# Loads of q and k: a fourth buffer, and issue 1.6 steps earlier

## The chip, the core and the metric

The kernel runs on one core of one Trainium2 chip. The metric is the device time of one execution in microseconds, as the median of several runs. Five engines work side by side, each with its own instruction queue in order: TensorE (PE, with its weight loads PEld), VectorE (DVE), ScalarE (ACT), GpSimd (POOL) and SyncE (SP), which computes nothing here and issues the plain transfers between HBM and the on-chip memory. Engines wait for one another through semaphores.

## The reference, cut to what matters

Attention in two forms is added up, and its result goes through a layer of eight experts, of which each token uses one.

```python
q, k, v: [8 batches, 8 heads, 576 tokens, 64]
q_d, k_d, v_d = means over 4 neighbouring tokens          # 144 tokens
out_d   = softmax(q_d k_d^T / 8) v_d, each row repeated 4 times
out_loc = softmax(q k^T / 8, only where |i - j| < 4) v
x = (out_d + out_loc) as [4608 tokens, 512]
e = argmax(x w_gate + bias);  out[t] = gate[t] * relu(x[t] w1[e]) w2[e]
```

## The kernel before

**Attention.** The work is cut into 32 steps (`N = 4 * B`), one for each pair of heads of a batch: step n is batch n // 4, pair n % 4. A step transposes q and k on PE (`tp`, line 278; `tpt`, line 291, for the remainder of two steps together), copies them on ACT (`qT`, `kT`), computes the banded scores in blocks (`sc`, line 341) and the pooled scores (`scd`, line 368), takes maxima and sums on DVE, exponentials on ACT and the normalizing products on POOL (`nl`, line 395; `nd`, line 399). The weights are transposed (`pdt`, line 417, on PE; `lt` on DVE) and multiplied with v: `avd` (line 431) with the pooled v, `avl` (line 446) with v itself. The pooled v comes from `vp` (line 266) on PE, once for two steps. `X` (line 457) adds both parts on DVE.

**Routing.** After each batch but the last, gate logits, the argmax and each token's place in a table are computed (`Router`), the table is written by indirect transfers of POOL (`scatter`, line 603), and the rows of x are turned by DVE (`R`, line 588) and stored to a buffer xs in HBM by SP (`store`, line 597). From the first four batches a first unit of 512 tokens is gathered while attention still runs (`entries`, line 834; `gather`, line 844).

**Experts.** From about 280 us on the experts' matrix products follow (lines 892 and 940), with weights loaded by SP (`wload`, lines 794 and 796).

**The order of the work** is written out by hand. Each operation has a phase in the table `PHASE`, in steps: operation x of step n is due at n + PHASE[x], so `vp` of step 4 is due at 4 + 2.4192. `build` collects all calls with their due times through `call(at, f, ...)`, sorts them by due time, and issues them in that order under a manual schedule; each engine works through its own instructions in this order. A due time is thus a place in an order, not a time on a clock.

**The loads.** `load_qk` (line 225) loads q and k of four heads of one batch, two steps' worth, with number h = 2 * batch + half: two transfers for q and two for k, 288 KB each, in rows of 256 bytes, all issued by SP at line 234. Its tiles `qt` and `kt` each hold 9 x 2 x 64 words a partition and rotate through a number of buffers; a load waits until the transposes that read the old content of its buffer are done. The loads h = 0, 1 and 2 stand ahead of everything; h = 3 to 15 come from the schedule (line 1022). `load_v` (line 237) loads v of four heads of the next batch into one of two v tiles, as four transfers of 192 KB (line 254), two such halves a batch (line 1020). SP also issues two fills of buffers in HBM at the start (`Router.start`, due at step 2.55: `xs<-zr` at line 476 and `tab<-ft`, 324 KB, at line 480) and the stores of the rows of x. All these stand in one queue, SP's.

The due times of SP's work around the change, with `last` = 0.1888 and `used` = 3.5377: v's halves of batch b+1 at 4b + 2.84 and 4b + 3.64, load h of q and k at 2h - 4.56, the stores of batch b at 4b + 8.17, 4b + 8.55 and 4b + 10.55.

Of the kernel before, what the change touches and what calls it, by code (L numbers as in the profile page):

```python
# [7 lines left out]
F32 = mybir.dt.float32  # L8
# [9 lines left out]
B, H, S, D = 8, 8, 576, 64  # L18
# [178 lines left out]
class Attention:  # L197
# [27 lines left out]
    def load_qk(s, b, half):  # L225
        nc = s.nc

        qt = s.ld.tile([128, 9, 2, D], F32, name="qt", bufs=3)
        kt = s.ld.tile([128, 9, 2, D], F32, name="kt", bufs=3)
        for j in (slice(0, 5), slice(5, 9)) if (b, half) == (0, 0) else (slice(0, 9),):  # L230
            for t, src in ((qt, s.q), (kt, s.k)):
                for a in range(2):
                    h = src[b, 4 * half + 2 * a : 4 * half + 2 * a + 2].rearrange("h s d -> (h s) d")
                    nc.sync.dma_start(t[:, j, a], h.rearrange("(j p) d -> p j d", p=128)[:, j])
        s.QK[2 * b + half] = (qt, kt)
# [717 lines left out]
def build(tc, q, k, v, mid, w_gate, bias, w1, w2, out):  # L953
    nc = tc.nc
    with ExitStack() as ctx:
# [8 lines left out]
        with ExitStack() as actx:  # L964
# [6 lines left out]
            at = Attention(tc, actx, ectx, C, ps, q, k, v)  # L971
# [27 lines left out]
            def call(at, f, *args):  # L999
                calls.append((at, len(calls), f, args))  # L1000
# [3 lines left out]
            last = max(P["tpq"], P["tpk"], P["tpt"])  # L1004
# [14 lines left out]
                    for j in range(2):  # L1019
                        call(4 * b - 1 + used + 0.3 + 0.8 * j, at.load_v, b + 1, 4 * j)  # L1020
            for h in range(3, N // 2):
                call(2 * h - 5 + last + 0.25, at.load_qk, h // 2, h % 2)


            call(0.95, C.sums, nc)
# [202 lines left out]
```

## Time and profile before

| What | us |
|---|---|
| runs before: median of 3 | 731.39 |
| runs before: lowest, highest | 731.2, 736.78 |
| the profiled execution: its own time | 737.82 |
| its span in the trace | 735.8 |
| busy in the span: PE | 670.7 |
| DVE, ACT, POOL | 381.1, 358.3, 296.9 |

The profile is of one execution. The span runs from its first to its last instruction. "Busy" is the time in which an engine works on an instruction; the durations of PE's products are modelled, and they overlap. In a row of the timeline there stand the start in us, the duration, the engine ("SPq" for a transfer that SP issues, with the time that the issuing takes), the line, the operation, what it writes and reads, and how many instructions were merged; in brackets follows the idle time before it and what ended this. The rows of stretches give the busy time of each engine in the stretch, the clock granted to PE as a share of full speed, the mean busy share of the sixteen DMA engines, and the rate.

### The profile page before, as it was taken

The numbers are of one execution on the slowest core, as the hardware profiler recorded it, in microseconds if no ns is written. First come the engines' busy times: TensorE is split into PE (matmuls) and PEld (weight loads), VectorE is DVE, ScalarE is ACT, GpSimd is POOL, SyncE is SP. The second block draws the span as 40 slices with busy tenths as digits, with TensorE's granted clock in tenths as the row PEclk, the third lists the DMA queues.
The fourth block names the chain that finished last, engine by engine and source line by source line (L and its number), as shares of the span: only waits on it lengthen the run. The fifth ranks groups of instructions, "written<-read, shape, count | busy, mean of one in ns | idle before, by whom it ended". The sixth has DMA issues, their size and how long they took to land. (4 is left out here: it accounts for less than half of the span.)

```text
span 735.8 us, 19186 instructions
## 1 busy us (share of the span) xinstructions
PE 670.7 (91%) x7467; PEld 540.8 (73%) x7467; DVE 381.1 (52%) x877; ACT 358.3 (49%) x804; POOL 296.9 (40%) x390
## 2 busy tenths in 40 slices
PE   6899989898869788894999999999999999999994
PEld 4677767676747566683788888888888888889793
DVE  3578778597737596650743423435224353235720
ACT  3688778676646474530443432434314343235620
POOL 6757585657767658066313132131412102211101
PEclk9899999999988999997899999999999999999998
DMA  9899778798997936936356253561635424344800
GB/s 177 159 188 169 175 153 176 143 192 181 175 169 126 163 85 131 299 95 184 129 135 210 61 145 138 141 203 46 187 112 155 160 78 146 106 144 139 252 14 28
DMA packets 175711, 107.92 MB, mean 147 GB/s; under 512 B 135582, under 2 KB 154050, under 8 KB 175619
## 3 DMA queue, kind: packets, MB, share of 16 engines
q1 hardware_dynamic: 167362, 87.45, 51.6%
q0 software_dynamic: 8256, 19.22, 8.4%
q8 instruction: 60, 0.98, 0.7%
q14 instruction: 33, 0.26, 0.1%
HBM read 87.39 MB, written 19.51 MB: 145 GB/s over the span
## 5 line engine op out<-in xcount | busy, mean ns | idle before, releaser
L944 POOL DMA_INDIRECT out_dram<-o,tg x37 | 40.1, 1083 | 258.9 <-ACT o L943 210.5
L821 DVE TENSOR_TENSOR wlo<-raw,whi 128x1024 fp32r<-128x1024 f32 x72 | 86.8, 1234 | 92.8 <-ACT whi L815 89.1
L897 DVE SCALAR_TENSOR_TENSOR hl<-l,hh 128x512 fp32r<-128x512 f32 x72 | 49.7, 690 | 106.6 <-ACT hh L896 104.2
L940 PE MATMUL l<-whi,hh 128*128 128x512 f32 x256 | 100.3, 396 | 0.0
L940 PE MATMUL l<-whi,hl 128*128 128x512 f32 x256 | 99.7, 390 | 0.0
L940 PE MATMUL l<-wlo,hh 128*128 128x512 f32 x256 | 99.6, 390 | 0.0
L896 ACT ACTIVATE hh<-l 128x512 fp32r<-128x512 f32 x72 | 42.6, 597 | 117.1 <-PE l L892 106.7
L892 PE MATMUL l<-xh,whi 128*128 128x512 f32 (+1 forms) x256 | 96.0, 377 | 2.1 <-DVE mni L623 1.1
L892 PE MATMUL l<-xl,whi 128*128 128x512 f32 (+1 forms) x256 | 95.2, 372 | 0.0
L892 PE MATMUL l<-xh,wlo 128*128 128x512 f32 (+1 forms) x256 | 95.0, 372 | 0.0
L815 ACT CAST whi<-raw 128x1024 fp32r<-128x1024 f32 x70 | 70.7, 1050 | 30.1 <-issue 12.0
L943 ACT ACTIVATE o<-l,tg 128x512 f32<-128x512 f32 x37 | 25.4, 687 | 110.4 <-PE l L940 58.2
L341 PE MATMUL sc<-kT,qT 64*24 64x32 f32 x3072 | 45.4, 194 | 16.9 <-issue 16.3
L411 ACT COPY Pw<-lt 32x288 f32<-32x288 f32 x128 | 54.6, 426 | 8.8 <-DVE lt L406 6.7
L341 PEld LDWEIGHTS sc<-kT,qT 64*24 64x24 f32 x3072 | 35.1, 100 | 31.4 <-issue 26.7
L892 PEld LDWEIGHTS l<-xh,whi 128*128 128x128 f32 x256 | 48.3, 189 | 12.2 <-issue 3.4
L940 PEld LDWEIGHTS l<-wlo,hh 128*128 128x128 f32 x256 | 48.1, 188 | 10.2
L603 POOL DMA_INDIRECT tab<-ig,si x36 | 37.9, 1053 | 42.8 <-DVE mbase L738 17.8
L940 PEld LDWEIGHTS l<-whi,hh 128*128 128x128 f32 x256 | 48.0, 188 | 9.6
L940 PEld LDWEIGHTS l<-whi,hl 128*128 128x128 f32 x256 | 48.1, 188 | 9.5
L892 PEld LDWEIGHTS l<-xl,whi 128*128 128x128 f32 x256 | 48.5, 190 | 8.3 <-issue 0.4
L892 PEld LDWEIGHTS l<-xh,wlo 128*128 128x128 f32 x256 | 48.5, 190 | 8.3
(246 smaller groups left out, 1315.0 us busy)
## 6 DMA issues: line engine op xcount, KB each, us to landing
raw<-in_moe_w_dram SPq DMA_DIRECT2D x176, 128.0 KB
raw<-in_moe_w_dram SPq DMA_DIRECT2D x44, 512.0 KB
vw<-in_v_dram SPq DMA_DIRECT2D x53, 192.0 KB
qt<-in_q_dram SPq DMA_DIRECT2D x30, 288.0 KB
kt<-in_k_dram SPq DMA_DIRECT2D x30, 288.0 KB
xs<-R SPq DMA_DIRECT2D x64, 128.0 KB
vw<-in_v_dram SPq DMA_DIRECT2D x15, 96.0 KB
xs<-R SPq DMA_DIRECT2D x12, 64.0 KB
```

Source lines behind the costliest of these rows:

```text
L341: s.nc.tensor.matmul(p[32 * j : 32 * j + SUB, i, :], qT[r, q0 : q0 + SUB], kT[r, q0 : q0 + WIN], start=False, stop=(i == NB - 1), skip_gro ...
L411: s.nc.scalar.copy(s.Pw[n % NPW][r, :, j, :SUB], s.t["lt", n][r, :, :SUB])
L603: i = nc.gpsimd.indirect_dma_start(out=s.tab[:, :], out_offset=bass.IndirectOffsetOnAxis(ap=C.si[:, t : t + 1], axis=0), in_=C.ig[:, t, :] ...
L815: (nc.gpsimd.tensor_copy if turn <= 4 else nc.scalar.copy)(hi, raw)
L821: (nc.gpsimd if 2 < turn <= 4 else nc.vector).tensor_tensor(lo, raw, hi.bitcast(F32), op=ALU.subtract)
L892: nc.tensor.matmul(p[:, f % n, :], a[:, fs], x[:, k, :N], start=(k == 0 and i == 0), stop=(k == 3 and i == 2))
L896: nc.scalar.activation(hh[:, g, :N], p, AF.Relu)
L897: nc.vector.scalar_tensor_tensor(hl[:, g, :N], p, 0.0, hh[:, g, :N].bitcast(F32), op0=ALU.max, op1=ALU.subtract)
L940: nc.tensor.matmul(p, a[:, f, hs], x[:, f % 2, :], start=(f == 0 and i == 0), stop=(f == 7 and i == 2))
L943: nc.scalar.mul(o, p, T[:, h, 1:2].bitcast(F32))
L944: nc.gpsimd.indirect_dma_start(out=s.out[:, :], out_offset=bass.IndirectOffsetOnAxis(ap=T[:, h, 0:1], axis=0), in_=o, in_offset=None, boun ...
```

## The change

`qt` and `kt` get four buffers each, and the due time of load h (h = 3 to 15) goes from 2h - 5 + `last` + 0.25 to 2h - 6.6 + `last` + 0.25. The transposes that use load h begin at step 2h. Nothing else is changed: the same transfers, of the same size, by the same engine.

```diff
     def load_qk(s, b, half):
         nc = s.nc
 
-        qt = s.ld.tile([128, 9, 2, D], F32, name="qt", bufs=3)
-        kt = s.ld.tile([128, 9, 2, D], F32, name="kt", bufs=3)
+        qt = s.ld.tile([128, 9, 2, D], F32, name="qt", bufs=4)
+        kt = s.ld.tile([128, 9, 2, D], F32, name="kt", bufs=4)
...
             for h in range(3, N // 2):
-                call(2 * h - 5 + last + 0.25, at.load_qk, h // 2, h % 2)
+                call(2 * h - 6.6 + last + 0.25, at.load_qk, h // 2, h % 2)
```

## Prediction

> **What bounds the kernel now.** I began with the page's busy shares and cut the attention stage (0 to 280 us) into stretches of 40 us, because the change touches only that stage. Columns: stretch, its length, busy time of PE, PEld, DVE, ACT and POOL with their instruction counts, granted clock, DMA share, GB/s.
>
> ```profile
> 40.00:80.00 40.00, 38.20 (x942) 30.02 (x940) 30.62 (x93) 32.29 (x98) 27.48 (x41) 1.00 0.92 170
> 80.00:120.00 40.00, 37.73 (x922) 29.25 (x917) 31.42 (x100) 30.95 (x98) 24.45 (x36) 1.00 0.80 172
> 200.00:240.00 40.00, 31.87 (x663) 24.94 (x658) 23.09 (x70) 23.00 (x70) 27.14 (x37) 0.83 0.83 149
> ```
>
> From 40 to 120 us PE has 1.8 and 2.3 us idle in 40: it sets the pace. The DMA engines are 80 to 92% busy beside it. So there are two limits that lie close together, and the question is whether PE ever waits for a load. The views of the tiles kt and of the line that pools v (L266) answer it with everything that PE waited for on loads in the whole attention stage; the tile qt shows no wait for a DMA.
>
> ```profile
>   DMA kt<-in_k_dram: 3.1, 1
> ...
>   DMA vw<-in_v_dram: 2.3, 1
> ```
>
> These are two waits. The timeline of PE places them, both in the first 20 us, on loads that the change leaves alone:
>
> ```profile
> 15.71 0.52 PE L278 MATMUL tp<-ident,kt 128*128 128x128 f32 x3 [3.11 <-DMA kt<-in_k_dram]
> ...
> 20.02 1.50 PE L266 MATMUL vp<-vw,pool 128*32 128x256 f32 x9 [2.33 <-DMA vw<-in_v_dram]
> ```
>
> Next the timeline of SyncE, which issues every load (start, duration, line, what, how many):
>
> ```profile
> 7.07 2.46 SPq L234 DMA_DIRECT2D kt<-in_k_dram  x2
> ...
> 12.81 3.60 SPq L254 DMA_DIRECT2D vw<-in_v_dram  x5
> ...
> 30.79 1.02 SPq L234 DMA_DIRECT2D qt<-in_q_dram  x2
> 31.91 3.85 SPq L234 DMA_DIRECT2D kt<-in_k_dram  x2
> 35.86 1.08 SPq L476 DMA_DIRECT2D xs<-zr  x1
> 37.04 0.59 SPq L480 DMA_DIRECT2D tab<-ft  x1
> 37.68 4.51 SPq L254 DMA_DIRECT2D vw<-in_v_dram  x4
> 42.29 3.08 SPq L234 DMA_DIRECT2D qt<-in_q_dram  x2
> 45.47 2.87 SPq L234 DMA_DIRECT2D kt<-in_k_dram  x2
> 48.39 4.50 SPq L254 DMA_DIRECT2D vw<-in_v_dram  x4
> ```
>
> The rows follow one another without a gap. SyncE is never ahead of its plan and waiting for a buffer; it is behind, and each issue takes as long as the queue needs to accept it. So in this stage **a place in the order of SyncE's queue is worth time, and a due time in steps is not**.
>
> **What the change moves.** Call a load of q and k "qk" with its number h (four transfers of 288 KB), and the two halves of v for batch b "vA(b)" and "vB(b)" (four transfers of 192 KB each). The largest of the three PHASE values that `last` takes is 0.1888, so a qk load was due at step 2h-4.56 and is now due at 2h-6.16. vA(b+1) is due at 4b+2.84, vB(b+1) at 4b+3.64, the fills of xs and tab at 2.55, the stores of the rows at 0.17, 0.55 and 2.55 of each four steps.
>
> qk3 goes from 1.44 to -0.16, but nothing else on SyncE stands between these, and it already follows directly on the loads of the constants: no change, cost nothing. qk4 goes from 3.44 to 1.84: it passes the two fills and vA(1), its four issues with it. In every later round the even qk passes a row store and vA, the odd qk passes two row stores. vB keeps the same set of transfers ahead of it. The added buffers mean 9 KB more a partition (two of 9x2x64 words), and a wait for buffer h-4 instead of h-3. The buffer was free long before in either case: qk4 was issued at 42.29 although its old buffer's last transposes belong to step 3, done before 32 us.
>
> **Gain of having q and k earlier: nothing.** The only wait for them that the trace shows is the one at 15.71, which stays. Bound: 0 from both sides, since a load that nobody waits for can't be made worth more.
>
> **Cost of having vA later.** How long does a load take from the end of its issue until PE can use it? Two rows tell it: the kt load issued until 7.07+2.46 = 9.53 let PE go at 15.71, 6.2 us later; the group of v that ended by 12.81+3.60 = 16.41 let PE go at 20.02, 3.6 us later. vA(1) is issued until 37.68+4.51 = 42.19, so it lands between 45.8 and 48.4. Its user is the v pooling of step 6:
>
> ```profile
> 47.68 1.06 PE L266 MATMUL vp<-vw,pool 128*32 128x256 f32 x12
> ```
>
> That row shows no wait, so the room is between 0 and 1.9 us. I take 0.5: vA(1) follows large transfers (288 KB, and tab's 324 KB), as the kt load did, not small ones as the first v did, and is nearer to the 6.2.
>
> qk4 occupies the queue from 42.29 to 48.39, 6.1 us. With it ahead, vA(1) lands 6.1 us later and **PE waits 6.1 - 0.5 = 5.6 us at about 48 us** (4.2 to 6.1). PE works in order: behind the v pooling stand avd, scd, avl and the second scores of step 6, hence ACT's Od and exp, DVE's lm and X. All engines lose the same time.
>
> **The clock after it.** The closest case is PE's wait of 5.16 us at 213.83:
>
> ```profile
> 213.83 1.52 PE L417 MATMUL pdt<-ident,de 128*96 128x128 f32 x6 [5.16 <-POOL de L399]
> 215.13 0.37 PE L332 MATMUL sc<-mask,identb 128*128 128x192 bf16 x1
> 215.29 1.06 PE L278 MATMUL tp<-ident,qt 128*128 128x128 f32 x4
> ...
> 228.28 0.86 PE L417 MATMUL pdt<-ident,de 128*96 128x128 f32 x6
> ...
> 229.21 0.60 PE L278 MATMUL tp<-ident,qt 128*128 128x128 f32 x4
> ```
> ```profile
> 193.70:197.10 3.40, 2.93 (x14) 2.82 (x15) 0.89 (x2) 1.09 (x3) 3.13 (x6) 0.50 1.02 170
> 213.80:217.60 3.80, 3.77 (x20) 3.21 (x24) 2.45 (x7) 1.66 (x5) 3.44 (x5) 0.50 1.04 220
> ```
>
> After the wait the granted clock is 0.50 for 3.8 us: six pdt take 1.52 instead of 0.86, four transposes of q 1.06 instead of 0.60, and four of k as much again. Loss 0.66 + 0.46 + 0.46 = **1.6 us** (0 to 1.6). The page "TensorE: Matmul & The Clock Gate" of the Trainium skill (section "What's actually happening") says that half clock comes after at least one idle window of about 3.4 us; by it the short end of the stall, 4.2 us, need not hold a whole window and would cost no clock. The other half-clock row here follows an idle of only 2.2 us:
>
> ```profile
> 194.17 1.52 PE L417 MATMUL pdt<-ident,de 128*96 128x128 f32 x6 [2.20 <-POOL de L399]
> ```
>
> So the trace is stricter than the rule, and I keep the 1.6.
>
> **The later rounds.** The same reckoning for vA(3) and vA(4), the tightest ones:
>
> ```profile
> 90.15 3.94 SPq L254 DMA_DIRECT2D vw<-in_v_dram  x4
> 94.19 1.60 SPq L234 DMA_DIRECT2D qt<-in_q_dram  x2
> ...
> 102.46 5.19 SPq L254 DMA_DIRECT2D vw<-in_v_dram  x4
> ...
> 122.93 2.86 SPq L254 DMA_DIRECT2D vw<-in_v_dram  x4
> 125.89 3.77 SPq L234 DMA_DIRECT2D qt<-in_q_dram  x2
> ...
> 134.77 6.29 SPq L254 DMA_DIRECT2D vw<-in_v_dram  x4
> ```
> ```profile
> L266 PE MATMUL vp<-vw,pool x12: 376/379/403, 107.4 to 108.1; 128*32 128x256 f32 x12
> ...
> L266 PE MATMUL vp<-vw,pool x12: 376/379/403, 137.5 to 138.2; 128*32 128x256 f32 x12
> ```
>
> vA(3): issued until 94.1, plus the 8.3 us of qk8, plus 3.6 to 6.2, is 106.0 to 108.6 against a use at 107.4. vA(4): 125.8 + 8.9 + 3.6 to 6.2 = 138.3 to 140.9 against 137.5, late by 0.8 to 3.4. But by then PE is 5.6 us behind its old times while the queue, which does not wait for PE, is not: both are covered, and cost nothing. Without that cover they cost 0 to 1.2 and 0.8 to 3.4 us. The stall at 48 us therefore buys the room for all later rounds; and were it made up meanwhile, vA(4) would still hold PE back.
>
> **What is won back.** Early: PE idles 1.8 + 2.3 = 4.1 us between 40 and 120; if the other engines run ahead during the stall, some of that can close. Most of it is lockstep, so 1 us (0 to 4.1). Late: near 210 us POOL waits 6.0 us for a scatter that lands slowly beside the full queue, and PE shows gaps with no releaser near 220:
>
> ```profile
> POOL tg L834 <- DMA tab<-ig,si: 6.0, 1, 6.0
> ...
> 219.75 0.28 PE L341 MATMUL sc<-kT,qT 64*24 64x32 f32 x4 [0.51 <-issue]
> ```
>
> The queue's last v issues end at about 221; with PE some 6 us later this work meets an emptier queue. I take 1.5 us (0 to 4, two thirds of the scatter's wait).
>
> **Sum:** +5.6 + 1.6 - 1.0 - 1.5 = **+4.7 us**. Ends: 4.2 + 0 - 4.1 - 4 = -3.9, and 6.1 + 1.6 = +7.7. From 280 us on the expert stage follows the attention in one chain, so the loss is carried to the end. Against the profiled execution's own 737.82 us (span 735.8) that gives 742.5. That execution is 6.4 us above the median of the runs shown, 731.39, like one of these (736.78); to the median the same sum gives **736.1 us**.
>
> **Rivals.**
>
> A, the room holds: not slower, 731.4. The mechanism is the queue's lead over PE at step 6: vA(1) may land 6.1 us later without harm where the whole queue stands further ahead of PE than in this profile. It decides from a lead that is 4.2 us longer than here (landing at 47.68 - 6.1 = 41.6 of the old times, against 45.8 at best). Against it: the first 40 us are issued back to back, with nothing to shorten. For it: the profiled execution is itself 6.4 us above the median, and some of that may sit here. Chance 0.14. The page "DMA: Bandwidth & Descriptors" of the Trainium skill (section "Rules for kernel authors") advises to issue a DMA early, to compute meanwhile and to wait for it late; by it an earlier q and k can only help, which here means 731.4 at best, as the trace shows no wait for them after 15.71.
>
> B, faster: the qk loads are out of the queue earlier, SyncE catches up before 200 us and the scatter lands at once; the 5.16 us of PE and the 1.6 us of clock go, with no stall at 48: 731.4 - 6.8 = 724.6. Against it: ahead of the last row stores and v loads stands the same set of transfers as before, so the queue is as full at 209. Chance 0.08.
>
> C, more than one stall: if the queue slows together with PE, because the row stores wait for DVE's rows, vA(3) and vA(4) are late again: 5.6 + 1.6 + 0.6 + 2.1 = +9.9, 741.3. For it: every vA loses a place. Against it: SyncE is about a step behind its plan, so rows are ready. Chance 0.20.
>
> D, the change does not do what it says, in that q and k are no earlier, since the queue and not the due time sets their issue. The order of calls is the order of SyncE's rows, so I give it no chance of its own beyond qk3, where it is true.
>
> **How the numbers follow.** My forecast has 0.58, with its own range of 731 to 739. One per cent, 7.3 us, is about what a measurement of this kernel can tell from no change. Slower by more: C nearly whole (0.17) and the upper end of the forecast (0.10), 0.27. Faster by more: half of B and something unseen, 0.09. Within: 0.64. The range reaches from 728 (the sum's low end is 727.5) to 742 (C).
>
> **What would show it.** In the changed profile the four issues of qk4 stand ahead of the fills of xs and tab; the L266 row of step 6 carries a wait of 4 to 6 us for a DMA of vw, with a half-clock stretch behind it; no later L266 row waits more than 1 us; steps 7 to 24 begin some 5 us later than before; the transposes of q and k still wait for no load after 20 us. Wrong would be: no wait at the L266 row of step 6, or a span that shrinks while that wait is there.

## The result, and the profile after

| | before | with the change |
|---|---|---|
| median of 20 runs, us | 731.93 | 735.62 |
| lowest, highest | 722.34, 736.78 | 733.57, 741.51 |

The ratio is 1.0086, with a 95% interval of 1.0059 to 1.0113; it leaves out the runs more than 1.5% above the fastest run of the same kernel, which are nine of the 20 before and none of the change's, so it is larger than the quotient of the medians of all runs (1.0050). The change makes the kernel slower, by 0.5% by these medians and 0.9% by the ratio; in the repetition further down both agree on 0.8%. The forecast was 736.1 us.

SyncE's timeline of the changed kernel around the first moved load (start, duration, line, what, how many):

```profile
30.04 1.07 SPq L234 DMA_DIRECT2D qt<-in_q_dram  x2
31.15 3.12 SPq L234 DMA_DIRECT2D kt<-in_k_dram  x2
34.38 3.46 SPq L234 DMA_DIRECT2D qt<-in_q_dram  x2
37.94 2.82 SPq L234 DMA_DIRECT2D kt<-in_k_dram  x2
40.85 1.16 SPq L476 DMA_DIRECT2D xs<-zr  x1
42.10 0.58 SPq L480 DMA_DIRECT2D tab<-ft  x1
...
42.74 4.79 SPq L254 DMA_DIRECT2D vw<-in_v_dram  x4
```

qk4 (34.38 to 40.76) now stands ahead of the fills and of vA(1). vA(1) begins to issue at 42.74 where it began at 37.68: 5.1 us later. Its first user is the `vp` of step 4, due at 6.42 and therefore called the v pooling of step 6 here. PE's timeline shows what becomes of it:

```profile
46.83 0.63 PE L341 MATMUL sc<-kT,qT 64*24 64x32 f32 x48
51.66 1.93 PE L266 MATMUL vp<-vw,pool 128*32 128x256 f32 x12 [4.20 <-DMA vw<-in_v_dram]
53.52 1.23 PE L431 MATMUL avd<-PdT,vd 96*64 96x144 f32 x8
54.68 1.38 PE L368 MATMUL scd<-kd,qd 64*64 64x144 f32 x12
...
58.44 0.60 PE L278 MATMUL tp<-ident,qt 128*128 128x128 f32 x4
```

The v pooling of step 6, which had no wait before, waits 4.20 us for v. Its own work then takes 1.93 us instead of 1.06. Stretches of PE around it, with the granted clock third from the end:

```profile
48.80:51.60 2.80, 0.00 (x0) 0.00 (x0) 0.00 (x0) 0.10 (x1) 1.09 (x2) 0.50 0.81 159
51.60:55.60 4.00, 3.94 (x28) 2.34 (x30) 0.00 (x0) 0.72 (x3) 0.22 (x1) 0.50 1.24 225
55.60:60.00 4.40, 4.40 (x108) 3.67 (x108) 3.72 (x11) 3.05 (x11) 0.95 (x3) 1.00 1.21 218
```

The clock is at one half from 48.8 us, within the wait, and for 4 us after it. From the start of the pooling to the next transposes of q it takes 58.44 - 51.66 = 6.8 us. In the profile of before the same stretch runs from 47.68 to these transposes:

```profile
52.65 0.60 PE L278 MATMUL tp<-ident,qt 128*128 128x128 f32 x4
```

That was 5.0 us. So the stretch behind the wait takes 1.8 us more, which the half clock would explain (the filler below tests this), and wait and stretch together lose 6.0 us. The 40 us that hold both read accordingly:

```profile
40.00:80.00 40.00, 34.06 (x823) 26.42 (x823) 26.85 (x84) 27.23 (x85) 22.23 (x33) 0.91 1.01 184
```

PE is busy for 34.1 us in 40 where it was for 38.2. The loads do not stand still with it: the eight issues of vA(1) and vB(1) end at 51.5 us, where in the kernel before vB(1), behind the same set of transfers, ended at 52.9. The v poolings of batches 3 and 4, at 114.57 and 143.28, wait for nothing:

```profile
114.57 1.06 PE L266 MATMUL vp<-vw,pool 128*32 128x256 f32 x12
...
143.28 1.06 PE L266 MATMUL vp<-vw,pool 128*32 128x256 f32 x12
```

### The profile page after: what moved, and what is told of

It is laid out like the page before. It is cut to its first block, busy times and chain, and to the rows that moved or that the text cites. A ratio compares the mean times of both kernels' runs of the same rounds, so it can differ in the third digit from the quotient of the medians.

```text
span 733.5 us, 19178 instructions
## 1 busy us (share of the span) xinstructions
PE 671.2 (92%) x7467; PEld 541.1 (74%) x7467; DVE 381.7 (52%) x877; ACT 358.4 (49%) x804; POOL 298.4 (41%) x390
```

## The experiments

The theory: the loss is one wait, since vA(1) has no room at step 6 and stands behind one more load of q and k. The rivals: the buffers themselves; a small loss at each displaced half of v; a loss elsewhere, with the wait made up later. Each kernel was timed beside the kernel before on the same chip; the four of the first group shared one set of runs of it (median 725.40), the next four another (727.22), the last two a third (725.25).

**Four buffers alone.** The new due time is taken back, the buffers stay.

```diff
-                call(2 * h - 6.6 + last + 0.25, at.load_qk, h // 2, h % 2)
+                call(2 * h - 5 + last + 0.25, at.load_qk, h // 2, h % 2)
```

> Four buffers for q and k, with the old due times: SyncE's order is that of the kernel before. Theory (the loss is the first half of v for batch 1 standing behind one more load of q and k): the same time as before, within 0.3%, and no wait of the v pooling at step 6. Rival (the buffers themselves cost, by the memory's layout or other waits): slower by about 0.9%, as the whole change.

Ratio 1.0032 (1.0001 to 1.0063), median 726.88. The interval leaves out 1 by a hair and lies below 1.0086: the buffers are not what costs the whole 0.9%, though a loss of a few tenths of a per cent isn't excluded by this kernel alone. Its profile shows how little room step 6 has even with the old order:

```profile
47.74 1.06 PE L266 MATMUL vp<-vw,pool 128*32 128x256 f32 x12 [0.43 <-DMA vw<-in_v_dram]
```

A wait of 0.43 us: the expectation of none was wrong here, and in this profile there was no room at all.

**Only load 4 early.**

```diff
-                call(2 * h - 6.6 + last + 0.25, at.load_qk, h // 2, h % 2)
+                call(2 * h - (6.6 if h == 4 else 5) + last + 0.25, at.load_qk, h // 2, h % 2)
```

> Four buffers, and only load h = 4 is issued early; loads 5 to 15 keep their old due times. Theory: this alone gives the whole loss, +3 to +5 us on the kernel before, with a wait of the v pooling of about 4 us at 48 us. Rival (every half of v that lost its place adds a little): less than +1.5 us.

Ratio 1.0088 (1.0058 to 1.0118), median 733.14. One moved load of thirteen gives the whole loss, and its wait:

```profile
51.77 1.93 PE L266 MATMUL vp<-vw,pool 128*32 128x256 f32 x12 [4.70 <-DMA vw<-in_v_dram]
```

By medians the loss is 7.7 us, by the ratio 6.4: both above the 3 to 5 that were expected.

**All but load 4 early.**

```diff
-                call(2 * h - 6.6 + last + 0.25, at.load_qk, h // 2, h % 2)
+                call(2 * h - (5 if h == 4 else 6.6) + last + 0.25, at.load_qk, h // 2, h % 2)
```

> The change, but load h = 4 keeps its old due time, so the first half of v for batch 1 stands where it stood. Theory in its simple form: no wait at step 6; but later halves of v have lost their places with no stall that covers them, so the pooling of batch 4 (step 18) waits 1 to 3 us: 0 to +2 us on the kernel before. Rival (all loads matter alike): +3 us or more.

Ratio 0.9995 (0.9964 to 1.0025), median 726.22. Twelve of the thirteen moved loads cost nothing that can be measured, and gain nothing; the interval spans 2.2 us on each side. This kernel too has four buffers. In its profile the pooling of step 6 has no wait, and that of batch 4 has the one that was expected of it:

```profile
47.03 1.06 PE L266 MATMUL vp<-vw,pool 128*32 128x256 f32 x12
...
136.62 1.06 PE L266 MATMUL vp<-vw,pool 128*32 128x256 f32 x12 [1.22 <-DMA vw<-in_v_dram]
```

In the change that wait is absent: PE gets to this pooling at 143.28, later by more than the wait.

**The cost doubled.** Both halves of v for batch 1 also stand behind load 5.

```diff
-                        call(4 * b - 1 + used + 0.3 + 0.8 * j, at.load_v, b + 1, 4 * j)
+                        call(4 * b - 1 + used + 0.3 + (1.04 + 0.02 * j if b == 0 else 0.8 * j), at.load_v, b + 1, 4 * j)
```

> The change, with both halves of v for batch 1 placed behind load h = 5 as well, so that the suspected cost is doubled. Theory: the pooling of step 6 waits 9 to 11 us in place of 4.2, and the time is 5 to 7 us above that of the change (+9 to +11 on the kernel before). Rival (the wait at step 6 is made up later, and the loss comes from elsewhere): the time of the change, within 2 us.

Ratio 1.0128 (1.0093 to 1.0163), median 735.17, which is 9.8 us above before. The wait is what the theory says:

```profile
57.27 1.07 PE L266 MATMUL vp<-vw,pool 128*32 128x256 f32 x6 [10.30 <-DMA vw<-in_v_dram]
```

Above before the loss is in the expected 9 to 11 us. The other half of the expectation, 5 to 7 us above the change, was missed: against the kernel with load 4 alone, in the same group, it is 2 us by the medians and 2.9 by the ratios (whose intervals leave 3 to 4 us either way), where the wait grew by 5.6. The doubled cost shows in the profile, and only partly in the times; by the medians the difference is about as small as the rival had it.

**v first again.** The change, with the first half of v due 1.2 steps earlier in every round.

```diff
-                        call(4 * b - 1 + used + 0.3 + 0.8 * j, at.load_v, b + 1, 4 * j)
+                        call(4 * b - 1 + used + (0.3 + 0.8 if j else -0.9), at.load_v, b + 1, 4 * j)
```

> The change, but the first half of v for each batch is due 1.2 steps earlier, so that it stands ahead of the even load of q and k again. Theory: no wait of the v pooling after 20 us, and the time of the kernel before, within 0.4% (it may gain a little, since batch 1's half of v now stands ahead of the fills too). Rival (q and k early cost by themselves, or the loss lies in the other transfers): slower than before by 0.5% or more.

Ratio 0.9989 (0.9956 to 1.0023), median 726.25: the loss is gone with the due times of q and k as in the change. On the queue load 4 is issued from 40.19 us now, 2.1 us sooner than before, where the change had it at 34.38. SyncE's order and the pooling of step 6:

```profile
34.41 5.68 SPq L254 DMA_DIRECT2D vw<-in_v_dram  x4
40.19 1.99 SPq L234 DMA_DIRECT2D qt<-in_q_dram  x2
```
```profile
47.66 1.06 PE L266 MATMUL vp<-vw,pool 128*32 128x256 f32 x12
```

vA(1) is issued 3.3 us sooner than in the kernel before, and nothing is gained by it: PE needs it at 47.7, not earlier. No order tried is measurably faster than before.

**Pooling later, with and without the change.** The due times of `vp` and `vc` move behind other work of PE; in the change, and in the kernel before as its control.

```diff
-"vp": 2.4192
+"vp": 3.0000
...
-"vc": 2.6555
+"vc": 3.1500
```

> The change, with the v pooling and its copy due 0.58 and 0.49 steps later, so that PE has about 4 us of other work ahead of the late load. Theory (the loss comes from PE's order, since everything behind the pooling waits with it): the wait of about 4 us falls below 1 us and the time goes back to that of its control without the change (the next kernel), within 0.4%. Rival (the load is late by itself, whatever PE does): slower than its control by 0.6% or more.

> The kernel before, with the v pooling and its copy due 0.58 and 0.49 steps later: the control of the kernel with the change and the same later pooling. Theory: within 0.5% of before; it may gain 1 to 2 us, as the wait of 2.3 us at 20 us falls away too.

With the change 1.0147 (1.0110 to 1.0185), without it 1.0152 (1.0108 to 1.0197). Beside its control the change costs nothing any more: the two ratios differ by 0.05%, with some 0.6% either way. The pooling of step 6, now at 53.59 in the change, has no wait, and step 7 begins almost alike, first with the change and then without it:

```profile
52.54 0.60 PE L278 MATMUL tp<-ident,qt 128*128 128x128 f32 x4
```
```profile
52.29 0.60 PE L278 MATMUL tp<-ident,qt 128*128 128x128 f32 x4
```

That is 0.25 us apart, where the change with the old pooling was 5.8 us late. The late load costs something only where PE comes to its user before it has landed.

The later pooling costs 1.5% by itself, against the expectation of at most 0.5% or a small gain. avd waits 1.92 us for the pooling's copy at 41 us in both profiles, but this is not where the 1.5% is lost, as step 7 of the control at 52.29 is no later than in the kernel before (52.65). It is 137.75 us at its step 18, against 132.6 to 134.3 with the old pooling and no late load. Over the whole kernel PE waits longer for POOL's `de`: 11.4 us in all in the profile of before, 18.9 in that of the control. Why `de` comes later wasn't traced, so the cause of the 1.5% stays open.

**Filler under the wait.** 16, then 24 products of zeros are put on PE just ahead of the pooling of step 6; nothing of the result is computed by them.

```diff
             call(2.05, C.routing, tc, cp, work, ps)
+            call(4 + P["vp"] - 0.001, C.busy, nc, 24)
```

> The change, with 16 products of zeros on PE just ahead of the v pooling of step 6, in which nothing of the result is computed. They fill about 3.5 us of the wait. Theory (the half clock after the wait costs 1 to 2 us): the granted clock stays whole around 50 us, step 7 starts 1 to 1.5 us earlier than in the change's profile, the time 0 to 2 us below the change. Rival (the clock costs nothing, only the wait does): step 7 starts as in the change's profile or later.

> The change with 24 products of zeros just ahead of the v pooling of step 6 (about 5.3 us, with 16 the wait still had 2.5 us of idle time left and the clock was halved after it). Theory (half clock comes from the idle time): the wait is below 1 us, the granted clock stays whole up to 190 us, and from the start of the pooling to the next transposes it takes 5.0 us as before, not 6.8; the time is 0 to 2 us below the change. Rival: the clock falls all the same, and the time is that of the change or more.

With 16 the time was 1.0042 (1.0013 to 1.0070), but its profile still has 2.45 us of idle time ahead of the pooling and half clock after it, and step 7 begins at 59.54, later than in the change and not 1 to 1.5 us earlier. This profile is of the longest of the twelve executions (737.34 us), and in it vA(1) begins to issue at 44.83, 2.1 us later than in the change's, so what the filler did can't be told from it. With 24 the profile does what was expected:

```profile
46.54 5.35 PE L126 MATMUL bz<-dummy 128*128 128x512 bf16 x24
51.90 1.06 PE L266 MATMUL vp<-vw,pool 128*32 128x256 f32 x12
...
56.88 0.60 PE L278 MATMUL tp<-ident,qt 128*128 128x128 f32 x4
```
```profile
51.90:56.80 4.90, 4.90 (x111) 3.78 (x112) 2.26 (x6) 2.57 (x11) 1.09 (x2) 1.00 1.03 202
```

The clock stays whole and the stretch takes 5.0 us, as before, though the load is as late as in the change: the 1.8 us come with PE's idle time and not with the late load. The time, 1.0080 (1.0060 to 1.0099), is that of the change; 1.8 us is a quarter of a per cent, and these intervals are 0.2% wide on each side, so the times neither show nor exclude it.

**The change once more.**

> The change once more, on the chip and beside the runs of before that the next kernel has, with a second profile. Theory: +5 to +7 us on before (0.7 to 1.0%), as the wait and the half clock of its first profile add up to 5.9 us and the other profiles show nothing of it won back; the pooling of step 6 waits 3.5 to 5 us and no later pooling waits. Rival (part is won back later, as the sum of the prediction had it): +3 to +4 us.

Ratio 1.0082 (1.0061 to 1.0104), median 730.76 against 725.25: 5.5 us by medians, 5.9 by the ratio. The wait at step 6 is 5.10 us in this profile, a little above the 3.5 to 5 expected, and no later pooling waits. The transposes of steps 7, 18 and 31 tell whether the loss is won back. First the change:

```profile
58.41 0.60 PE L278 MATMUL tp<-ident,qt 128*128 128x128 f32 x4
...
138.26 0.60 PE L278 MATMUL tp<-ident,qt 128*128 128x128 f32 x4
...
251.41 0.60 PE L278 MATMUL tp<-ident,qt 128*128 128x128 f32 x4
```

Then with v first:

```profile
52.63 0.60 PE L278 MATMUL tp<-ident,qt 128*128 128x128 f32 x4
...
132.59 0.60 PE L278 MATMUL tp<-ident,qt 128*128 128x128 f32 x4
...
242.85 0.60 PE L278 MATMUL tp<-ident,qt 128*128 128x128 f32 x4
```

5.8 us late at step 7, 5.7 at step 18, 8.6 at step 31. One pair of profiles is not enough for the last figure, as the others show. Four profiles have vA(1) ahead of load 4 (before, buffers alone, all but load 4, v first), three have it behind (the change twice, load 4 alone):

| Transposes of q begin, us | vA(1) ahead | vA(1) behind | means apart by |
|---|---|---|---|
| step 7 | 52.0 to 52.7 | 58.4 to 58.5 | 5.9 |
| step 18 | 132.6 to 134.3 | 138.3 to 140.4 | 6.0 |
| step 31 | 242.9 to 257.7 | 251.4 to 258.4 | 5.9 |

Up to step 18 nothing is won back by the means, though single pairs lie 4.0 to 7.8 us apart. At step 31 the kernels of one group differ by up to 15 us among themselves, so the profiles can't tell a recovery of 1 or 2 us there. From step 31 to the end all seven take 474 to 478 us: what is lost by then stays lost.

## Why the prediction was right, point by point

**Order, not time, on SyncE's queue: right.** Load 4 alone makes the loss, the other twelve make none, and putting vA ahead of it takes the loss away.

**No gain from q and k earlier: right.** With all loads but one early, and with v first, the time is that of before within 0.4%.

**The wait, 5.6 us (4.2 to 6.1): right in place and mechanism, a little too large.** It measured 4.20, 4.70 and 5.10 us in three profiles with load 4 ahead of vA(1), 10.30 with two loads ahead, 0.43 in one with the old order and none in the others. In the three, vA(1) begins to issue 5.1, 5.5 and 5.9 us later than before, where the sum had 6.1, and each wait is 0.8 to 0.9 us shorter than that, where the sum had 0.5 for the room. The room is no fixed number, as the time from the end of the issue until PE can go varies: 5.5 us with the buffers alone (issued from 37.62 to 42.23, PE at 47.74), 4.1 in the change (47.53 to 51.66).

**The clock, 1.6 us: right.** The stretch behind the wait is 1.8, 1.7 and 1.6 us longer in the three profiles, and with the wait filled it isn't. How long PE has to idle for it is not settled by these traces: in the profile of before, half clock goes with the idle time of 2.20 us that ends at 194.17, and the clock stays whole (1.00 from 120 to 160 us) around one of 2.31 us that ends at 136.54.

**Later rounds covered: right.** None of the later poolings waits in the change; without the early stall the one of batch 4 does, 1.22 us against the 0.8 to 3.4 worked out.

**Won back, 2.5 us: too large, if there is anything.** The early part, 1.0, is not to be seen: the lag of 5.9 us at step 7 is 6.0 at step 18. The late part, 1.5, was to come from the scatter near 210 us, which would meet an emptier queue. POOL's wait for it in the first profile of the change, and in the profile with v first:

```profile
POOL tg L834 <- DMA tab<-ig,si: 4.6, 1, 4.6
```
```profile
POOL tg L834 <- DMA tab<-ig,si: 5.5, 1, 5.5
```

Its longest wait is 4.6, 4.8 and 5.2 us with load 4 ahead of vA(1), and 5.1 to 6.0 in the four profiles without: 0.7 us shorter by the means. Wait and stretch together lose 6.0, 6.4 and 6.7 us at step 7, and the ratios of the same kernels (1.0086, 1.0088, 1.0082) come to 6.3, 6.4 and 5.9 us at the end. So about nothing is won back by the middle values, but each ratio has an interval of some 2 us either way. With v behind two loads step 7 is about 12 us late and the times lose 9.3 (ratio) to 9.8 us (medians); a recovery behind a longer stall isn't excluded.

So the nearness of the forecast is in part luck. The loss itself was put at 7.2 us, some 0.5 to 1.2 too high, and a recovery of 2.5 that hardly came was taken off it. The quotient of the first medians, +3.7 us, would suit the +4.7 better than the ratio's +6.3, but the second pair of medians, +5.5, does not.

**The rivals.** A (room) is excluded by the waits. B (an emptier queue late) is worth 0.7 us of the scatter's wait and does not outweigh the stall. C (more than one stall) did not happen: no later pooling waits in the three profiles with load 4 ahead, and the issues of vB(1) end 1.4 us sooner than before while PE stands still. A sign of being wrong that the prediction names, a span that shrinks while the wait is there, is met by the two first profiles (735.8 us before, 733.5 with the change), but the execution profiled before took 737.82 us where the medians are 731.93 and 735.62, so these two spans say nothing of the change. The page "DMA: Bandwidth & Descriptors" of the Trainium skill (section "Rules for kernel authors") advises to issue early; the runs here show the other side of it where the issues follow one another without a gap, as the load issued early pushed back one whose user was due sooner.

**Open.** The four buffers alone measured 1.0032 with an interval that just leaves out 1. Two other kernels with four buffers lose nothing (0.9995 and 0.9989), which speaks against a cost of the buffers, but neither has the old order. The time between steps 18 and 31, which differs by up to 15 us between profiles of kernels that measure alike, was not explained. Three buffers with the early due times weren't tried, since a load would stand ahead of the transposes that still read its buffer.

## What to carry to other kernels

Where the transfers of one queue follow one another without a gap, an earlier due time moves a load forward only by moving others back: list what it passes, and look for the one with the least room between landing and first use. A deeper buffer pays only where its user waits. And a wait of an in-order engine can cost more than its length: here 4.2 to 5.1 us of wait carried 1.6 to 1.8 us of half clock, and none of it had come back 80 us later.

## What was not expected

Moving the v pooling by half a step, in a kernel whose stall it was to hide, cost 1.5% (1.0152, with the old loads), and the wait that shows first, 1.92 us of avd at 41 us, is not where it was lost. And the room of vA(1) at step 6 was so small that the old order waits for it in one profile, 0.43 us, and not in another. Last, a cost of 0.8% that the times show plainly can't be read from one pair of profiles at step 31, as the kernels of one group differ by more than that there.
